# One token tile through a precomputed low-rank product, fewer and longer unread matmuls, and later values: one change in three parts to an attention-and-mixer kernel

## The chip, the cores and the metric

The kernel runs on one core of a Trainium2 chip. The metric is the device time of one execution in microseconds (us), as a median over several executions. Before the change it is 313.06 us (three runs, 312.72 to 313.33). All times below that come from a trace are counted from the first instruction of the profiled execution. The trace's span is about 1.7 us shorter than the device time of the same execution (311.4 for 313.08).

## The reference

Sliding-window causal attention, then a mixer with a low-rank product over the tokens and a two-layer MLP over the channels:

```python
# q, k, v: (8, 8, 576, 64); window 64
scores = scale * q @ k.T                       # masked to 0 <= i - j < 64
x = softmax(scores) @ v                        # -> (8, 576, 512)
xt = x.transpose(0, 2, 1)
h = xt @ U @ V                                 # U: (576, 32), V: (32, 576)
u = x + h.transpose(0, 2, 1)
out = u + np.maximum(u @ w_ch1, 0.0) @ w_ch2   # 512 -> 2048 -> 512
```

The 576 tokens of a batch are handled as five tiles, four of 128 tokens and one of 64.

## The kernel before

The MLP needs u with the channels on the partitions ("d-major"), and the last addition needs it with the tokens on the partitions. For batch 0 the d-major u is made on TensorE in four PSUM banks, one for 128 channels each: XT transposes x into them and HT adds the low-rank product. `hh` is U'x, made by UM in one bank (`psh` for batch 0, `pshh` for the others) and cast by ScalarE.

```python
def UM(ts):                                    # hh = U' x over the token tiles ts
    def f():
        ...                                    # tiles 0-3: two matmuls each, two column groups
        ...                                    # tile 4: four matmuls, each half the columns
        if ts[-1] == NT - 1:
            hh["sb"] = wk_pool.tile([P, CH], BF16, name="hh", tag="hh")
            for cs in (slice(0, CH // 2), slice(CH // 2, CH)) if spare else (slice(0, CH),):
                nc.scalar.copy(out=hh["sb"][:, cs], in_=hh["ps"][:, cs])
    return f

def bank(dc):                                  # the PSUM bank of channel block dc
    if dc not in ua:
        if dc < 2:
            ua[dc] = psum["mm"].tile([P, CH], FP32, name="uam", tag="mm")[:]
        elif dc == 2:
            ua[dc] = ps_tp.tile([P, CH], FP32, name="uat", tag="tp")[:]
        else:
            ua[dc] = ps_big.tile([P, 2, CH], FP32, name="uab", tag="big")[:, 0, :]
    return ua[dc]

def HT(dcs):                                   # called with (0, 1), then (2, 3)
    def f():
        for n, dc in enumerate(dcs):
            half = slice(n * 2 * R, (n + 1) * 2 * R)
            nc.tensor.matmul(bank(dc), hh["sb"][half, dc * P : (dc + 1) * P],
                             vrep[half, W : W + CH], start=False, stop=True)
        for dc in dcs:
            copy = nc.scalar.copy if dc % 2 == 0 else nc.vector.tensor_copy
            copy(out=uT_of(b)[:, :, dc, :], in_=bank(dc).rearrange(...))
    return f
```

The program begins with matmuls whose results nobody reads. They are there to raise TensorE's clock while the first loads are under way (its record goes from half to full at 6.03 us in this trace). Then come batch 0's attention and mixer, and from then on the MLP of one batch with the attention and mixer of the next one spread over its numbered slots:

```python
PLACE_0 = {"V": [0, 0, 1, 2, 2, 3, 4, 4, 4]}   # batch 0's token-major values of u (psv)
PLACE_1 = {..., "SV": [18, 18, 19, 19], "PV": [20], "U": [25], "V": [26, 31], ...}
...
turn_over(62, 96)                              # 62 unread matmuls of 96 columns
...                                            # batch 0: scores, head tiles
a["R"](); ...                                  # values of tiles 0, 1
a["PV"][2](); spread_v(3, nc.scalar.copy)
a["XT"][0](); a["XT"][1]()
a["PV"][3](); a["U"][0]()
a["PV"][4](); a["U"][1]()
for t in range(2, NFULL):
    a["XT"][t](); a["U"][t]()
for f in [a["U"][NT - 1]] + a["X3"] + a["HT"]:
    f()
```

SV copies batch 1's V into place, PV computes its attention values, U its hh.

The softmax here doesn't subtract the row's maximum and nothing guards it: scores larger than these inputs give would overflow.

Of the kernel before, what the change touches and what calls it, by code (L numbers as in the profile page):

```python
# [11 lines left out]
BF16 = mybir.dt.bfloat16  # L12
FP32 = mybir.dt.float32
# [3 lines left out]
def kernel(  # L17
# [11 lines left out]
    nc = tc.nc  # L29
    B, H, S, D = q.shape  # L30
    DM = H * D
    R = moe_U.shape[1]
    F = moe_w_ch1.shape[1]
    P = nc.NUM_PARTITIONS
    W = 64
    NB = S // W
    HP = H // 2
    NDC = DM // P
# [7 lines left out]
    NFULL = S // P  # L46
    CH = 512
# [11 lines left out]
    const = ctx.enter_context(tc.tile_pool(name="const", bufs=1))  # L59
# [3 lines left out]
    wk_pool = ctx.enter_context(tc.tile_pool(name="wk", bufs=2))  # L63
# [17 lines left out]
    NT = 5  # L81
# [2 lines left out]
    vrep = const.tile([P, W + S + W], BF16, name="vrep")  # L84
    vf = const.tile([R, S], FP32, name="vf")
    idle = const.tile([P, CH], BF16, name="idle")
    xs = [const.tile([P, NT, H, D], BF16, name=f"xs{i}") for i in range(2)]
    vA = [const.tile([P, NFULL, H, VW], BF16, name=f"vA{i}") for i in range(2)]
    vB = [const.tile([P, NFULL, H, VW], BF16, name=f"vB{i}") for i in range(2)]
# [60 lines left out]
    def shift_low(b, copy, t):  # L150
# [9 lines left out]
        out=ident[:],  # L160
        in_=ident[:],
# [27 lines left out]
    nc.vector.memset(vrep[:, W + S : W + S + W], 0.0)  # L189
    nc.vector.memset(uf[0][:, NT - 1, :], 0.0)  # L190
    nc.vector.memset(xs[0][W:P, NT - 1, :, :], 0.0)
    nc.vector.memset(xs[1][0:W, 0, :, :], 0.0)
    for i in range(2):
        nc.vector.memset(kn[i][GP:P, NFULL, :, :], 0.0)
# [27 lines left out]
    def spread_v(g, copy):  # L222
        copy(out=vrep[g * R : (g + 1) * R, W : W + S], in_=vf[:])
# [8 lines left out]

    def load_rest():
        load_w1(1024, 2048)
        for g in range(3):
            spread_v(g, nc.gpsimd.tensor_copy)
        for _ in load_kq(1, False):
            pass
        w2v = moe_w_ch2.rearrange("(i p) m -> p i m", p=P)
        for i in range(0, NFC, 4):  # L240
            if i == NFC - 4:
                load_v(1)
            nc.gpsimd.dma_start(out=w2b[:, i : i + 4, :], in_=w2v[:, i : i + 4, :])
# [10 lines left out]
    def attention(b, spare=False):  # L254
# [262 lines left out]
        hh = {}  # L517
        xc = lambda src, t, dc: src[:, t, :, :].rearrange("p h d -> p (h d)")[:, dc * P : (dc + 1) * P]

        def UM(ts):  # L520
            def f():
                if ts[0] == 0:
                    if spare:
                        hh["ps"] = psum["spare"].tile([P, CH], FP32, name="psh", tag="spare")
                    else:
                        hh["ps"] = ps_big.tile([P, 2, CH], FP32, name="pshh", tag="big")[:, 0, :]
                for t in ts:
                    xt = x[:, t, :, :].rearrange("p h d -> p (h d)")
                    if t < 4:
                        for g in (t % 2, t % 2 + 2):  # L530
                            nc.tensor.matmul(  # L531
                                hh["ps"][g * R : (g + 1) * R, :], ub[odd][:, t, :], xt,
                                start=(t < 2), stop=False,
                            )
                        continue

                    for g in range(4):
                        cols = slice((g % 2) * CH // 2, (g % 2 + 1) * CH // 2)
                        nc.tensor.matmul(  # L539
                            hh["ps"][g * R : (g + 1) * R, cols], ub[odd][:, t, :], xt[:, cols],  # L540
                            start=False, stop=True,
                        )
                if ts[-1] == NT - 1:
                    hh["sb"] = wk_pool.tile([P, CH], BF16, name="hh", tag="hh")
                    for cs in (slice(0, CH // 2), slice(CH // 2, CH)) if spare else (slice(0, CH),):
                        nc.scalar.copy(out=hh["sb"][:, cs], in_=hh["ps"][:, cs])  # L546
            return f


# [3 lines left out]
        def bank(dc):  # L553
            if dc not in ua:
                if dc < 2:
                    ua[dc] = psum["mm"].tile([P, CH], FP32, name="uam", tag="mm")[:]
                elif dc == 2:
                    ua[dc] = ps_tp.tile([P, CH], FP32, name="uat", tag="tp")[:]
                else:
                    ua[dc] = ps_big.tile([P, 2, CH], FP32, name="uab", tag="big")[:, 0, :]  # L560
            return ua[dc]

        opened = []
# [13 lines left out]
        def XT(t, dcs):  # L577
            def f():
                opened.append(t)
                for dc in dcs:  # L580
                    cols = bank(dc)[:, t * P : (t + 1) * P]

                    nc.tensor.matmul(cols, xc(x, t, dc), ident[:], start=(t == 0), stop=False)
            return f

        def HT(dcs):
            def f():
                for n, dc in enumerate(dcs):
                    half = slice(n * 2 * R, (n + 1) * 2 * R)
                    nc.tensor.matmul(  # L590
                        bank(dc),
                        hh["sb"][half, dc * P : (dc + 1) * P],
                        vrep[half, W : W + CH],
                        start=False,
                        stop=True,
                    )
                for dc in dcs:
                    copy = nc.scalar.copy if dc % 2 == 0 else nc.vector.tensor_copy
                    copy(  # L599
                        out=uT_of(b)[:, :, dc, :],  # L600
                        in_=bank(dc).rearrange("p (t q) -> p t q", q=P),
                    )
            return f
# [63 lines left out]
            pcs["M"] = [MK(j) for j in range(HP)]  # L667
            pcs["M"].insert(0 if b >= NGR else HP, MK8)
        pcs["PV"] = [PVA] if not spare else [None, None] + [PV(t) for t in range(2, NT)]
        pcs["U"] = [UM((t,)) for t in range(NT)] if spare else [UM(tuple(range(NT)))]  # L670
        if spare:
            pcs["L"] = [PVL(t) for t in range(2)]
            pcs["R"] = PVR
            pcs["XT"] = [XT(t, range(NDC - 1)) for t in range(NFULL)]
            pcs["idle"] = idle_turns
            pcs["X3"] = [XT(t, (NDC - 1,)) for t in range(NFULL)]
            pcs["HT"] = [HT((0, 1)), HT((2, 3))]
            pcs["V"] = [f for ts in ((0, 1), (2, 3), (4,)) for f in VM(ts)]
        else:
            def two_banks():  # L680
                return (
                    psum["mm"].tile([P, CH], FP32, name="psv0", tag="mm"),
                    ps_tp.tile([P, CH], FP32, name="psv1", tag="tp"),
                )

            def mixed(parts=None):
                parts = parts or [VM((NT - 1,), two_banks), VM((0, 1)), VM((2, 3))]
                for part in parts:
                    part[0]()
                for part in parts:  # L690
                    for add in part[1:]:
                        add()

            pcs["V"] = [mixed]
            if b == 1:

                def last():
                    for f in VM((NT - 1,)):
                        f()

                pcs["V"] = [lambda: mixed([VM((0, 1)), VM((2, 3))]), last]
            pcs["UT"] = [UT(t) for t in range(NT if odd else NT - 1)]
# [6 lines left out]
    def mlp(c):  # L709
# [83 lines left out]
        "V": [16],  # L793
        "UT": [17, 17, 18, 18, 19],
    }
    PLACE_0 = {"V": [0, 0, 1, 2, 2, 3, 4, 4, 4]}
    PLACE_1 = {
        "T": [11, 11, 12, 12, 14, 14, 15, 15],
        "S": [12, 13, 15, 16, 16],
        "M": [13, 14, 16, 17, 17],  # L800
        "SV": [18, 18, 19, 19],
        "PV": [20],
        "U": [25],
        "V": [26, 31],
        "UT": [28, 29, 30, 31, 102],
# [21 lines left out]
    def turn_over(n, cols, rows=P):  # L827
        for _ in range(n):
            nc.tensor.matmul(
                unread[0:rows, 0:cols], idle[:, 0:rows], idle[:, 0:cols], start=True, stop=True  # L830
            )


    turn_over(62, 96)
    att = {0: attention(0, spare=True)}
    a = att[0]
    nc.vector.tensor_scalar(
# [27 lines left out]
    for what in order.split():  # L865
        j = int(what[1])
        if what[0] in "SBL":
            a[what[0]][j]()
        else:
            a["T"][2 * j + (what[0] == "Q")]()  # L870
        if what == "Q1":
            load_low_rank()
            nc.scalar.copy(out=ub[0][:], in_=uf[0][:])
        if what in ("Q1", "Q3"):
            turn_over(1, CH)
    load_rest()
# [2 lines left out]
    shift_low(0, nc.scalar.copy, 2)  # L879
    a["idle"](1)  # L880
    a["PV"][2]()
    spread_v(3, nc.scalar.copy)
    a["XT"][0]()
    a["XT"][1]()
    a["PV"][3]()
    a["U"][0]()
    a["PV"][4]()
    a["U"][1]()
    for t in range(2, NFULL):
        a["XT"][t]()  # L890
        a["U"][t]()
    load_low_rank_1()
    for f in [a["U"][NT - 1]] + a["X3"] + a["HT"]:
        f()
    repeat(nc.vector.tensor_copy, maskA[:, 0])
    nc.vector.tensor_copy(out=maskA[:, 1, :, :], in_=maskA[:, 0, :, :])
# [7 lines left out]
    for c in range(NCH):  # L904
        slots = all_slots[c]

        def place(b, parts, where):
            if b not in att:
                att[b] = attention(b)
            for part in parts:  # L910
                for f, s in zip(att[b][part], where[part]):
                    all_slots[c + s // 100][s % 100].append(f)

        b = c + 1
        if b < B:
# [20 lines left out]
            if b < NXB:  # L936
                place(b, ("T",), where)
            if b == 1:
                place(0, ("V",), PLACE_0)
                slots[6].append(lambda: nc.scalar.copy(out=ub[1][:], in_=uf[1][:]))  # L940
            if 3 < b + 1 < B:
                slots[24].append(lambda bs=b + 1: shift_v(bs, nc.vector.tensor_copy))
# [57 lines left out]
```

## Time and profile before

| | before |
|---|---|
| median of 3 runs | 313.06 us |
| span of the trace | 311.4 us |
| TensorE (PE) busy | 303.9 us, 98% |
| first transposing product into u (XT) | 16.45 us |
| first low-rank product into u (HT) | 20.74 us |
| first MLP matmul (psA) | 21.80 us |
| batch 1's first pshh (U1) | 51.61 us |

The page says that TensorE is the limit; the five times are read from TensorE's timeline and are the milestones. Each stretch between two of them is a stage. Two lines of TensorE's waits in the first 64 us (for whom it waited; us in total, times, longest) show that in the stage before psA there were two waits of 0.4 us, one on ScalarE's cast of u and one on nothing that the profile shows ("issue"):

```profile
PE psA L724 <- ACT uTc L599: 0.4, 1, 0.4
PE psh L539 <- issue: 0.4, 1, 0.4
```

ScalarE's timeline of the kernel before (start, us, instruction) has the two copies of V on which batch 0's value tile 3 depends; they end at 16.79:

```profile
15.49 0.62 ACT L148 COPY vB<-vA 64x520 bf16<-64x520 bf16 x1
16.17 0.62 ACT L151 COPY vB<-vA 64x520 bf16<-64x520 bf16 x1
```

### The profile page before, as it was taken

How to read it: one execution, taken by the hardware profiler on the slowest of the kernel's cores; microseconds unless marked ns; L12 is line 12 of the kernel's file. 1: busy time of each engine (PE TensorE's matmuls, PEld its weight loads, DVE VectorE, ACT ScalarE, POOL GpSimd, SP SyncE). 2: the span in 40 equal slices, each digit the busy share in tenths (PEclk: the TensorE clock that was granted, in tenths of full speed). 3: DMA queues.
4: the chain of work that ended last, by engine and by line, in shares of the span. 5: the costliest groups of instructions: out<-in, count | busy, mean ns of one | idle time of the engine just before them, and what ended most of it. 6: DMA issues, size and time to landing. Idle time of an engine off the chain costs nothing.

```text
span 311.4 us, 6970 instructions
## 1 busy us (share of the span) xinstructions
PE 303.9 (98%) x2897; PEld 148.4 (48%) x2919; DVE 161.8 (52%) x308; ACT 108.8 (35%) x173; POOL 101.7 (33%) x133
## 2 busy tenths in 40 slices
PE   8989999999999999999999999999999999999996
PEld 7643554544455544453445344544454444444443
DVE  4665467437758753774368435844574343016011
ACT  3745670467038510642063304340345003201500
POOL 8693263293497097029308710000000000000000
PEclk9999999999999999999999999999999999999999
DMA  7999999999999999999999999515100545010012
GB/s 108 167 210 208 205 168 147 145 148 154 129 150 140 126 152 156 182 161 159 163 155 207 150 106 181 128 48 133 69 2 0 120 180 193 27 76 34 0 64 73
DMA packets 156496, 39.88 MB, mean 128 GB/s; under 512 B 145040, under 2 KB 151440, under 8 KB 156464
## 3 DMA queue, kind: packets, MB, share of 16 engines
q0 software_dynamic: 104720, 18.88, 87.3%
q1 hardware_dynamic: 51744, 20.55, 35.0%
q8 instruction: 23, 0.38, 0.5%
q14 instruction: 9, 0.07, 0.1%
HBM read 37.97 MB, written 9.44 MB: 152 GB/s over the span
## 4 chain that ended last, share of the span: by engine, by line
PE 93%; DMA 3%; POOL 2%; issue 1%; ACT 0%; DVE 0%; POOLq 0%
PE psA L724 41%; PE psU L748 40%; DMA vA<-in_v_dram 3%; PE sc L345 3%; PE xw L407 2%; PE psv L619 2%; PE pshh L531 1%; PE tpu L653 1%; PE tpg L281 0%; POOL qr L119 0%; PE low L345 0%; PE psh L531 0%; POOL vB L151 0%; PE xr L407 0%; POOL kr L119 0%
## 5 line engine op out<-in xcount | busy, mean ns | idle before, releaser
L724 PE MATMUL psA<-uTc,w1b 128*128 128x512 bf16 (+1 forms) x580 | 131.2, 378 | 0.4 <-ACT uTc L599 0.4
L748 PE MATMUL psU<-w2b,c 128*128 128x512 bf16 (+2 forms) x572 | 127.5, 373 | 1.3 <-issue 0.3
L748 PEld LDWEIGHTS <-c 128*128 128x128 bf16 x592 | 56.0, 98 | 66.4 <-issue 3.6
L724 PEld LDWEIGHTS <-w1b 128*128 128x128 bf16 x580 | 54.1, 98 | 64.4 <-issue 2.9
L736 ACT ACTIVATE c<-psA 128x512 bf16<-128x512 f32 x84 | 50.0, 597 | 88.3 <-PE psA L724 88.0
L761 DVE TENSOR_TENSOR osb<-psU,un 128x512 f32<-128x512 f32 (+2 forms) x29 | 19.5, 672 | 69.3 <-PE psU L748 69.3
L734 DVE TENSOR_SCALAR c<-psA 128x512 bf16<-128x512 f32 x60 | 41.3, 688 | 25.6 <-PE psA L724 25.6
L634 DVE TENSOR_TENSOR un<-psv,xs 128x512 bf16<-128x512 f32 (+3 forms) x48 | 26.1, 592 | 23.5 <-PE psv L619 23.3
L365 ACT ACTIVATE pts<-sc 128x1024 bf16<-128x1024 f32 x32 | 31.4, 1028 | 2.3 <-PE sc L345 2.3
L137 POOL DMA_DIRECT2D vA<-in_v_dram x32 | 28.5, 915 | 8.1 <-DMA w1b<-in_moe_w_ch_dram 2.8
L128 POOL DMA_DIRECT2D qr<-in_q_dram x30 | 26.7, 890 | 4.5 <-DMA w2b<-in_moe_w_ch_dram 3.1
L128 POOL DMA_DIRECT2D kr<-in_k_dram x30 | 26.7, 890 | 4.1 <-PE psA L724 2.0
L398 ACT ACTIVATE ptl<-low 128x256 bf16<-128x256 f32 x6 | 2.3, 384 | 62.0 <-PE high L345 62.0
L371 DVE TENSOR_TENSOR pts<-pts,maskA 128x1024 bf16<-128x1024 bf16 x28 | 19.1, 682 | 1.7 <-ACT pts L365 1.7
L922 POOL COPY held<-qf 1x1 bf16<-1x1 bf16 x5 | 1.1, 228 | 54.0 <-DMA qf<-qr 54.0
L498 DVE TENSOR_TENSOR xs<-xw,rcw 128x896 bf16<-128x896 f32 x14 | 15.3, 1091 | 0.5
L345 PEld LDWEIGHTS <-kf 64*64 64x64 bf16 x704 | 9.9, 107 | 7.7 <-issue 7.0
L345 PE MATMUL sc<-qf,kf 64*64 64x128 bf16 (+1 forms) x608 | 11.7, 212 | 0.5 <-DVE qf L298 0.3
L407 PEld LDWEIGHTS <-pts 128*64 128x64 bf16 x512 | 9.9, 110 | 3.7 <-issue 3.2
L546 ACT CAST hh<-pshh 128x512 bf16<-128x512 f32 x7 | 4.1, 586 | 13.7 <-PE pshh L539 13.5
L656 ACT COPY uTc<-tpu 128x512 bf16<-128x512 bf16 x9 | 5.3, 585 | 10.2 <-PE tpu L653 10.2
L407 PE MATMUL xw<-vA,pts 128*64 128x65 bf16 x217 | 8.4, 195 | 0.0
(115 smaller groups left out, 175.3 us busy)
## 6 DMA issues: line engine op xcount, KB each, us to landing
out_dram<-osb SPq DMA_DIRECT2D x27, 256.0 KB, 2.3
vA<-in_v_dram POOLq DMA_DIRECT2D x32, 128.0 KB, 8.1
kr<-in_k_dram POOLq DMA_DIRECT2D x24, 128.0 KB, 5.8
qr<-in_q_dram POOLq DMA_DIRECT2D x24, 128.0 KB, 6.4
w2b<-in_moe_w_ch_dram POOLq DMA_DIRECT2D x4, 512.0 KB, 15.0
out_dram<-late SPq DMA_DIRECT2D x8, 256.0 KB, 3.0
vB<-in_v_dram POOLq DMA_DIRECT2D x8, 128.0 KB, 12.3
w1b<-in_moe_w_ch_dram POOLq DMA_DIRECT2D x2, 512.0 KB, 11.5
```

The lines of the kernel that those rows point to most:

```text
L128: nc.gpsimd.dma_start(out=dst[0:rows, t, :, :], in_=src[b, :, t * P : t * P + rows, :].rearrange("h p d -> p h d"),)
L137: nc.gpsimd.dma_start(out=dst[:, :, 0:D], in_=v[b, :, lo : lo + P, :].rearrange("h p d -> p h d"))
L345: nc.tensor.matmul(sc[g][r0 : r0 + W, col * W : (col + n) * W], keys_of(j, u, rs), queries_of(j, blk, n, rs), start=not spare, stop=last o ...
L365: nc.scalar.activation(out=dst, in_=sc[:], func=ACT.Exp, scale=scale)
L371: nc.vector.tensor_tensor(out=dst, in0=dst, in1=maskA.rearrange("p g n w -> p g (n w)"), op=ALU.mult)
L407: nc.tensor.matmul(dst, pts[:, h // 2, h % 2, blk, :] if blk < NB - 1 else ptl[:, h // 2, h % 2, :], rhs, start=True, stop=True,)
L634: nc.vector.tensor_tensor(out=u_tiles[g][rs, cs], in0=ps[0][n][rs], in1=x[rs, t, :, :].rearrange("p h d -> p (h d)")[:, cs], op=ALU.add,)
L724: nc.tensor.matmul(ps[i][:, ts.start * P : ts.stop * P], w1b[:, dc, i * P : (i + 1) * P], uTc[:, ts, dc, :], start=(dc == 0), stop=(dc == ...
L734: nc.vector.tensor_relu(out=c1[i][:], in_=ps[i][:])
L736: nc.scalar.activation(out=c1[i][:], in_=ps[i][:], func=ACT.Relu)
L748: nc.tensor.matmul(acc[t][:, lo:hi], c1[i][:, t * P : (t + 1) * P], w2b[:, i, lo:hi], start=(i == 0), stop=(i == NFC - 1),)
L761: nc.vector.tensor_tensor(out=osb[:, lo:hi], in0=acc[t][:, lo:hi], in1=u_tiles[g][:, lo:hi], op=ALU.add,)
```

## The change

The intent is to start the MLP earlier. hh of batch 0's first four tiles no longer waits for the fifth, because the last tile's share of the low-rank product, its U times V, is made once from the weights alone (`m4`) and multiplied with the last tile of x. hh over all five tiles is still needed for the token-major values, so UM runs once more in the MLP's slot 0. The unread matmuls become fewer and longer, which leaves fewer instructions ahead of the kernel proper. Batch 1's values go one slot later.

```diff
-        def UM(ts):
+        def UM(ts, early=False):
...
+                if early and ts[-1] == NFULL - 1:
+                    hh["four"] = wk_pool.tile([P, CH], BF16, name="hh4", tag="hh4")
+                    for cs in (slice(0, CH // 2), slice(CH // 2, CH)):
+                        nc.scalar.copy(out=hh["four"][:, cs], in_=hh["ps"][:, cs])
...
-                elif dc == 2:
-                    ua[dc] = ps_tp.tile([P, CH], FP32, name="uat", tag="tp")[:]
                 else:
-                    ua[dc] = ps_big.tile([P, 2, CH], FP32, name="uab", tag="big")[:, 0, :]
+                    pair = ps_big.tile([P, 2, CH], FP32, name="uab", tag="big")
+                    ua[2], ua[3] = pair[:, 0, :], pair[:, 1, :]
...
+        def mix_last():
+            ps = ps_tp.tile([P, CH], FP32, name="psm", tag="tp")
+            for n in range(W // R):
+                rs = slice(n * R, (n + 1) * R)
+                nc.tensor.matmul(ps[rs, :], u4t[rs, :], vrep[rs, W : W + CH], ...)
+            nc.scalar.copy(out=m4[0:W, :], in_=ps[0:W, :])
...
         def HT(dcs):
...
-                        hh["sb"][half, dc * P : (dc + 1) * P],
+                        hh["four"][half, dc * P : (dc + 1) * P],
...
                 for dc in dcs:
+                    nc.tensor.matmul(
+                        bank(dc), xc(x, NT - 1, dc), m4[:], start=False, stop=True
+                    )
                     copy = nc.scalar.copy if dc % 2 == 0 else nc.vector.tensor_copy
...
-    PLACE_0 = {"V": [0, 0, 1, 2, 2, 3, 4, 4, 4]}
+    PLACE_0 = {"U": [0], "V": [2, 2, 3, 4, 4, 5, 6, 6, 6]}
...
-        "SV": [18, 18, 19, 19],
-        "PV": [20],
+        "SV": [19, 19, 20, 20],
+        "PV": [21],
...
-    turn_over(62, 96)
+    turn_over(40, 149)
...                                  # load_rest spreads V's copies in another order
-    a["U"][0]()
+    a["U4"][0]()
     a["PV"][4]()
-    a["U"][1]()
-    for t in range(2, NFULL):
-        a["XT"][t]()
-        a["U"][t]()
+    a["mix"]()
+    a["U4"][1]()
+    a["XT"][2]()
+    a["U4"][2]()
+    a["U4"][3]()
+    a["XT"][3]()
     load_low_rank_1()
-    for f in [a["U"][NT - 1]] + a["X3"] + a["HT"]:
+    for f in a["X3"] + a["HT"]:
         f()
```

The matmul added in HT is called a tail below.

More of the change, by code (lines that the diff above doesn't have):

```diff
@@ L86 @@
     idle = const.tile([P, CH], BF16, name="idle")
+    u4t = const.tile([W, R], BF16, name="u4t")
+    m4 = const.tile([P, CH], BF16, name="m4")
     xs = [const.tile([P, NT, H, D], BF16, name=f"xs{i}") for i in range(2)]
@@ L191 @@
     nc.vector.memset(xs[0][W:P, NT - 1, :, :], 0.0)
+    nc.vector.memset(m4[W:P, :], 0.0)
     nc.vector.memset(xs[1][0:W, 0, :, :], 0.0)
@@ L234, in load_rest @@
         load_w1(1024, 2048)
-        for g in range(3):
+        for g in (0, 2, 3):
             spread_v(g, nc.gpsimd.tensor_copy)
@@ L518, in attention @@
         xc = lambda src, t, dc: src[:, t, :, :].rearrange("p h d -> p (h d)")[:, dc * P : (dc + 1) * P]
-        def UM(ts):
+        def UM(ts, early=False):
             def f():
                 if ts[0] == 0:
-                    if spare:
+                    if early:
                         hh["ps"] = psum["spare"].tile([P, CH], FP32, name="psh", tag="spare")
@@ L532, in f @@
                                 hh["ps"][g * R : (g + 1) * R, :], ub[odd][:, t, :], xt,
-                                start=(t < 2), stop=False,
+                                start=(t < 2), stop=(early and t >= 2),
                             )
@@ L542, in f @@
                         )
+                if early and ts[-1] == NFULL - 1:
+                    hh["four"] = wk_pool.tile([P, CH], BF16, name="hh4", tag="hh4")
+                    for cs in (slice(0, CH // 2), slice(CH // 2, CH)):
+                        nc.scalar.copy(out=hh["four"][:, cs], in_=hh["ps"][:, cs])
                 if ts[-1] == NT - 1:
                     hh["sb"] = wk_pool.tile([P, CH], BF16, name="hh", tag="hh")
-                    for cs in (slice(0, CH // 2), slice(CH // 2, CH)) if spare else (slice(0, CH),):
-                        nc.scalar.copy(out=hh["sb"][:, cs], in_=hh["ps"][:, cs])
+                    nc.scalar.copy(out=hh["sb"][:], in_=hh["ps"][:])
             return f
@@ L584, in XT @@
             return f
+        def mix_last():
[3 more added lines that the diff above has]
+                nc.tensor.matmul(
+                    ps[rs, :], u4t[rs, :], vrep[rs, W : W + CH], start=True, stop=True
+                )
+            nc.scalar.copy(out=m4[0:W, :], in_=ps[0:W, :])
         def HT(dcs):
@@ L591, in f @@
                         bank(dc),
-                        hh["sb"][half, dc * P : (dc + 1) * P],
+                        hh["four"][half, dc * P : (dc + 1) * P],
                         vrep[half, W : W + CH],
                         start=False,
-                        stop=True,
+                        stop=False,
                     )
                 for dc in dcs:
+                    nc.tensor.matmul(
+                        bank(dc), xc(x, NT - 1, dc), m4[:], start=False, stop=True
+                    )
                     copy = nc.scalar.copy if dc % 2 == 0 else nc.vector.tensor_copy
@@ L669, in attention @@
         pcs["PV"] = [PVA] if not spare else [None, None] + [PV(t) for t in range(2, NT)]
-        pcs["U"] = [UM((t,)) for t in range(NT)] if spare else [UM(tuple(range(NT)))]
+        pcs["U"] = [UM(tuple(range(NT)))]
+        pcs["U4"] = [UM((t,), True) for t in range(NFULL)]
         if spare:
@@ L673, in attention @@
             pcs["R"] = PVR
-            pcs["XT"] = [XT(t, range(NDC - 1)) for t in range(NFULL)]
+            pcs["XT"] = [XT(t, (0, 1)) for t in range(NFULL)]
+            pcs["mix"] = mix_last
             pcs["idle"] = idle_turns
-            pcs["X3"] = [XT(t, (NDC - 1,)) for t in range(NFULL)]
+            pcs["X3"] = [XT(t, (2, 3)) for t in range(NFULL)]
             pcs["HT"] = [HT((0, 1)), HT((2, 3))]
@@ L873 @@
             nc.scalar.copy(out=ub[0][:], in_=uf[0][:])
+            nc.vector.transpose(out=u4t[:], in_=ub[0][0:W, NT - 1, :])
         if what in ("Q1", "Q3"):
@@ L881 @@
     a["PV"][2]()
-    spread_v(3, nc.scalar.copy)
+    spread_v(1, nc.scalar.copy)
     a["XT"][0]()
@@ L938 @@
             if b == 1:
-                place(0, ("V",), PLACE_0)
+                place(0, ("U", "V"), PLACE_0)
                 slots[6].append(lambda: nc.scalar.copy(out=ub[1][:], in_=uf[1][:]))
```

## The prediction

> **What bounds the kernel now.** I read the page first, then the chain of waits in order of time, then the timelines of TensorE, VectorE and ScalarE over the first 62 us.
>
> The page's busy times and its chain by engine:
>
> ```profile
> PE 303.9 (98%) x2897; PEld 148.4 (48%) x2919; DVE 161.8 (52%) x308; ACT 108.8 (35%) x173; POOL 101.7 (33%) x133
> ...
> PE 93%; DMA 3%; POOL 2%; issue 1%; ACT 0%; DVE 0%; POOLq 0%
> ...
> q8 instruction: 23, 0.38, 0.5%
> ```
>
> TensorE is busy 98% of the span and is 93% of the chain. So a matmul added after the start costs its full time, and there is little to win but the few idle pieces. The third line, the instruction queue, matters below.
>
> The chain in order of time, around the start (start, us, what):
>
> ```profile
> 6.16 7.85 DMA vA<-in_v_dram
> 14.06 0.61 POOL vB L151
> 14.73 0.62 POOL vB L148
> 15.40 0.62 POOL vB L151
> 16.07 0.45 PE xr L407 x16
> 21.18 0.58 ACT uTc L599
> 21.80 1.89 PE psA L724 x8
> ```
>
> Up to 16.07 the end is set by loading V and by three GpSimd copies, not by TensorE. From 21.80, when the first MLP matmul (psA) starts, TensorE is gapless. The change can act in the 5.73 us between, and through TensorE work or waits after them. The TensorE timeline of that stretch:
>
> ```profile
> 18.62 0.39 PE L531 MATMUL psh<-xs,ub 128*32 128x512 bf16 x2
> 18.94 0.28 PE L583 MATMUL uam<-ident,xs 128*128 128x128 bf16 x2
> 19.07 0.22 PE L583 MATMUL uat<-ident,xs 128*128 128x128 bf16 x1
> 19.21 0.39 PE L531 MATMUL psh<-xs,ub 128*32 128x512 bf16 x2
> 19.97 0.29 PE L539 MATMUL psh<-xs,ub 128*32 128x256 bf16 x4 [0.36 <-issue]
> 20.19 0.40 PE L583 MATMUL uab<-ident,xs 128*128 128x128 bf16 x4
> 20.74 0.39 PE L590 MATMUL uam<-vrep,hh 64*128 64x512 bf16 x2
> 21.02 0.39 PE L590 MATMUL uat<-vrep,hh 64*128 64x512 bf16 x1
> 21.02 0.39 PE L590 MATMUL uab<-vrep,hh 64*128 64x512 bf16 x1
> 21.80 1.89 PE L724 MATMUL psA<-uTc,w1b 128*128 128x512 bf16 x8 [0.40 <-ACT uTc L599]
> ```
>
> A pair of psh matmuls runs together and the next kind starts 0.32 after it (18.62 to 18.94). The last token tile's psh starts at 19.97, not at 19.21 + 0.32 = 19.53: 0.44 lost to "issue". Its input was ready, since VectorE ended that tile's xs at 18.51 + 0.68 = 19.19, and even its weight load, which waits for no semaphore, starts only at 19.97. In the compiled list this is PE row 703. Counting 64 rows of prologue (my guess) makes row 704 = 3 x 256 - 64 a fetch-block edge, so I read the 0.44 as waiting for instructions. Then the products uam wait for the cast hh, and psA for hh products and the cast uTc.
>
> **What the Trainium skill says.**
> - "Runtime: NRT & Kernel Launch", Instruction fetch mechanics: instructions come in 16 KiB blocks of 256, and crossing an edge is mostly hidden. The trace agrees on the size (0.38 MB in 23 fetches is 16.5 KB each). On hidden, this case differs once, by 0.44 us, if my reading holds.
> - "TensorEngine Tiling (Array Packing)", Key Properties: changing the tiling mode drains TensorE. The trace agrees: a pair of 512-column matmuls ahead of another shape takes 0.32 where one such matmul takes 0.216 (13.81 us for 64 psA on the chain), so about 0.1 per switch.
> - "TensorE: Matmul & The Clock Gate", What's actually happening: the array starts at half its 2.4 GHz. The 62 unread matmuls of 96 columns take 4.96 us (1.26 to 6.22), 80 ns each, which is 96 / 1.2 GHz: agrees.
>
> **The change part by part.**
>
> 1. *40 unread matmuls of 149 columns for 62 of 96.* 5,960 columns for 5,952: at half clock 4.97 us for 4.96, so the start stays. What it does do is take 44 rows out of TensorE's list, which moves the edge at row 704 from the early chain to the first re-done U matmul in MLP slot 0, reached some 3 us later. The 0.44 goes.
>
> 2. *Early chain from 16.07.* Walking the new list with the old steps:
>  - the transposing products XT of tiles 0 and 1 have 4 matmuls, not 6 (-0.11), but value tile 3 waits for a ScalarE copy ending 16.17 + 0.62 = 16.79, so it moves from 16.94 to 16.86 only: -0.08.
>  - The mixing product, two matmuls at once, adds 0.32.
>  - U of tiles 2 and 3 are now adjacent and use four column groups at once: -0.32.
>  - U of tile 4 is gone (0.22) and with it the 0.44.
>  - The ScalarE cast of the product now starts after tile 3's U (18.81 + 0.39, so about 19.25) and its first half is ready at 19.67, while TensorE does ten more XT until 19.79. The old wait 20.37 to 20.74 shrinks to one switch: -0.22.
>  - Then pair, two tail matmuls (0.22 each), pair, two tail matmuls: 19.79, 20.12, 20.34, 20.65, 20.97, 21.20, done issuing at 21.41. Four 512-column tail matmuls are the price (0.86) plus two switches.
>  - The first cast uTc runs 20.55 to 21.14, before TensorE needs it, so the old wait before psA (21.02 + 0.31 to 21.80, 0.47) is filled with work.
>  psA starts at about 21.41 for 21.80: **-0.39**. The later casts (21.46, 22.00, 22.31) are ahead of their matmuls (21.84, 22.27, 22.70).
>
> 3. *U of batch 0 done once more in slot 0* (8 + 4 matmuls), for the token-major values. The same group for batch 1 shows the cost:
>
> ```profile
> 50.65 1.03 PE L748 MATMUL psU<-w2b,c 128*128 128x512 bf16 x4
> 51.61 0.62 PE L531 MATMUL pshh<-xs,ub 128*32 128x512 bf16 x8
> 52.05 0.28 PE L539 MATMUL pshh<-xs,ub 128*32 128x256 bf16 x4
> 52.27 1.04 PE L748 MATMUL psU<-w2b,c 128*128 128x512 bf16 x4
> ```
>
>  Four psU from 50.65 would let the next start at 50.65 + 4 x 0.216 = 51.51; it starts at 52.27: **+0.75**, all on the path, as TensorE is gapless there.
>
> 4. *The first psv waits for hh.* psA pair ends issuing at 23.13, U at 23.88, psA 2 at 24.75; psv could start at 24.85. ScalarE evicts c 0 and 1 from 23.33 (1.0 for two, as 23.72 to 24.81 minus the tail), then casts hh until 24.91: psv at about 24.97, **+0.12**. Moving V from slots 0, 2, 4 to 2, 4, 6 costs nothing else.
>
> 5. *Batch 1's values one slot later (slot 21), while its U stays at slot 25.* VectorE's chain behind the values:
>
> ```profile
> 47.17 0.18 DVE L487 RECIPROCAL rce<-xe 128x4 f32<-128x4 f32 x1 [1.78 <-PE xe L407]
> ...
> 50.28 0.17 DVE L506 RECIPROCAL rco<-one 128x4 f32<-128x4 f32 x1
> 50.48 0.86 DVE L510 TENSOR_TENSOR xs<-one,rco 64x256 bf16<-64x256 f32 x2
> ```
>
>  It ends at 51.34, U's first matmul waits for exactly that last op (tile 0 of batch 1 is filled last) and starts at 51.61: with 0.05 for the semaphore there is 0.22 to spare. One slot less between values and U takes away four psU, 4 x 0.216 = 0.86. So a new wait of 0.86 - 0.22 = **+0.65**. What the move buys, more time for V's loads and copies, was worth nothing in this trace: values started at 45.90 with the usual switch gap.
>
> Sum: -0.39 + 0.75 + 0.12 + 0.65 = **+1.13 us**, 313.06 to 314.2.
>
> **Rivals.**
> - *The early gain carries.* If everything after psA absorbed the additions, the time would be 312.7. For it: the intent. Against: TensorE idles 0.32 us in all from 40 to 60 us (19.68 busy of 20), so 0.75 of new matmuls has nowhere to hide.
> - *The VectorE wait at batch 1's U does not come* (the wait is on an earlier op than I think, or the chain starts earlier): 313.5. Against: the compiled list has that matmul wait for VectorE, and the chain's order is unchanged.
> - *Instruction fetch becomes the wait elsewhere.* The edge now falls in slot 0; if the fetch is asked for only when the first psA is released (21.4), and takes the 2.3 us that it took before (17.64 to 19.97), up to 0.5 comes back: 314.7. Against: rows 664 to 703 are read some 2 us earlier than that.
> - *A load becomes the bound.* V of batch 1 lands at 45.06; with TensorE about 0.5 later and values a slot later it has 1.3 us more room. This makes no time, only less scatter.
>
> **Range and chances.** The two large terms, 0.75 and 0.65, are read from the same trace at nearly the same place; the early term rests on a walk of some fifteen steps, each good to a few hundredths, so +-0.3. The three runs before spread over 0.6 us. I take 314.2, with 313.2 to 315.0. Two per cent is 6.3 us, six times the largest sum I can form, so "within 2%" is near certain.
>
> **What would show it.** Right if: unread still ends near 6.22; no "issue" gap near 19.5; psA starts near 21.4; twelve pshh matmuls follow at about 23.2; the first psv waits about 0.1 on ScalarE; and pshh of batch 1 shows a wait of about 0.65 on VectorE's xs. From there to the end the distances should equal the old ones. Wrong if psA starts before 21.0 or after 21.8 (the walk missed a wait), if pshh of batch 1 shows no wait, or if an issue gap stands at slot 0.

## The result, and the profile after

The changed kernel takes **316.5 us** (six runs, 315.68 to 318.39) where the kernel before took 312.84 in six runs. A ratio here and below is the mean time of one kernel's fast runs over that of the other's of the same rounds, so it is not quite the ratio of the medians: 1.0124, with a 95% interval of 1.0093 to 1.0156. The class "within 2%" was right; the range 313.2 to 315.0 did not hold the time. The profiled execution is the fastest of the six, 315.68 us with a span of 314.0.

The page of the changed kernel, busy times and chain by engine: TensorE's own work has grown by 0.9 us only, and VectorE and ScalarE now stand in the chain with 1% each, where the page before gave them 0%.

```profile
PE 304.8 (97%) x2888; PEld 148.2 (47%) x2911; DVE 162.9 (52%) x310; ACT 110.0 (35%) x175; POOL 101.9 (32%) x133
PE 92%; DMA 2%; DVE 1%; ACT 1%; issue 1%; POOL 1%; POOLq 0%
```

The waits of TensorE in the first 64 us name three that the kernel before did not have:

```profile
PE uab L612 <- ACT uTc L616: 0.7, 1, 0.7
PE pshh L534 <- DVE xs L513: 0.6, 1, 0.6
PE xr L410 <- ACT vB L153: 0.3, 1, 0.3
```

The second was predicted (0.65). The others were not. TensorE's timeline of the same trace shows where they lie, and a small "issue" gap at the first head values:

```profile
14.51 0.22 PE L410 MATMUL xh<-vA,pts 128*64 128x65 bf16 x3 [0.23 <-issue]
...
17.41 0.19 PE L410 MATMUL xr<-vB,pts 128*64 128x65 bf16 x1 [0.33 <-ACT vB L153]
...
21.20 0.39 PE L604 MATMUL uab<-vrep,hh 64*128 64x512 bf16 x2
21.52 0.39 PE L612 MATMUL uab<-m,xs 128*128 128x512 bf16 x1
22.59 0.38 PE L612 MATMUL uab<-m,xs 128*128 128x512 bf16 x1 [0.67 <-ACT uTc L616]
22.80 1.89 PE L743 MATMUL psA<-uTc,w1b 128*128 128x512 bf16 x8
```

The two tails of the second HT are at 21.52 and 22.59, 1.07 apart where two adjacent ones are 0.22 apart. Between them lies ScalarE's cast of the bank that the first tail filled. ScalarE's timeline of the changed kernel: the cast runs from 21.95 to 22.53, and the second tail starts 0.06 later. The copy of V now ends at 17.35, and value tile 3 starts 0.06 after it.

```profile
15.47 0.60 ACT L401 ACTIVATE ptl<-sc 128x512 bf16<-128x512 f32 x1 [0.30 <-PE sc L348]
...
16.73 0.62 ACT L153 COPY vB<-vA 64x520 bf16<-64x520 bf16 x1
...
21.95 0.58 ACT L616 CAST uTc<-uab 128x512 bf16<-128x512 f32 x1 [0.27 <-PE uab L612]
```

The milestones of every trace, in us. "A to U1" is the stretch from the end of the last psA matmul of the first eight (0.22 after its start) to batch 1's first pshh; "edge" is the step from the matmul before to the one at row 447 to 449 of TensorE's compiled list. With 62 unread matmuls this is a change from one tiling of the array to another, and the same change takes 0.31 in all thirteen traces. With 40 or 50 it is in the middle of a group, whose matmuls otherwise follow each other within 0.05.

| kernel | unread | XT | XT to HT | HT to psA | psA | A to U1 | U1 to end | span | edge |
|---|---|---|---|---|---|---|---|---|---|
| before | 62 | 16.45 | 4.29 | 1.06 | 21.80 | 28.08 | 259.8 | 311.4 | 0.31 |
| before_again | 62 | 17.03 | 3.86 | 1.06 | 21.94 | 28.09 | 259.8 | 311.5 | 0.31 |
| after | 40 | 16.68 | 3.66 | 2.46 | 22.80 | 29.68 | 259.8 | 314.0 | 0.42 |
| after_again | 40 | 17.01 | 3.84 | 2.46 | 23.31 | 30.10 | 260.6 | 315.8 | 0.73 |
| a1_tails_first | 40 | 16.77 | 3.84 | 1.62 | 22.23 | 29.60 | 259.9 | 313.7 | 0.57 |
| a2_old_slots | 40 | 17.00 | 3.84 | 2.46 | 23.30 | 30.27 | 261.1 | 316.4 | 0.85 |
| a3_unread62 | 62 | 16.63 | 3.64 | 2.46 | 22.73 | 29.60 | 259.8 | 313.8 | 0.31 |
| a4_own_banks | 40 | 16.90 | 3.69 | 1.62 | 22.21 | 29.60 | 259.8 | 313.3 | 0.71 |
| b1_unread40 | 40 | 17.27 | 4.21 | 1.06 | 22.54 | 28.08 | 260.0 | 312.3 | 0.71 |
| b2_later_slot | 62 | 16.73 | 3.74 | 1.06 | 21.53 | 28.74 | 259.8 | 311.8 | 0.31 |
| b3_redo_u | 62 | 16.23 | 4.04 | 1.06 | 21.33 | 28.95 | 259.8 | 311.8 | 0.31 |
| b4_unread50 | 50 | 17.24 | 4.01 | 1.06 | 22.31 | 28.08 | 259.8 | 311.9 | 1.20 |
| c3_three_undone | 62 | 17.01 | 3.52 | 1.62 | 22.15 | 28.95 | 259.8 | 312.6 | 0.31 |

For the profiled pair: U1 is 2.60 later (54.21 for 51.61), and so is the end. That is 1.00 before psA and 1.60 between psA and U1. After U1 nothing has changed.

### The profile page after: what moved, and what is told of

It reads as the page before. It is cut to its first block, busy times and chain, and to the rows that moved or that the text cites. A ratio compares the mean times of both kernels' runs of the same rounds, so it can differ in the third digit from the quotient of the medians.

```text
span 314.0 us, 6958 instructions
## 1 busy us (share of the span) xinstructions
PE 304.8 (97%) x2888; PEld 148.2 (47%) x2911; DVE 162.9 (52%) x310; ACT 110.0 (35%) x175; POOL 101.9 (32%) x133
## 4 chain that ended last, share of the span: by engine, by line
PE 92%; DMA 2%; DVE 1%; ACT 1%; issue 1%; POOL 1%; POOLq 0%
PE psA L743 41%; PE psU L767 39%; PE sc L348 3%; DMA qr<-in_q_dram 2%; PE xw L410 2%; PE psv L636 2%; PE pshh L534 1%; PE tpu L670 1%; DVE xs L501 1%; PE tpg L284 1%; PE low L348 0%; POOL kr L121 0%; PE tpw L284 0%; PE psh L534 0%; PE xe L410 0%
## 5 line engine op out<-in xcount | busy, mean ns | idle before, releaser
L139 POOL DMA_DIRECT2D vB<-in_v_dram x8 | 7.4, 926 | 3.7 <-DMA qr<-in_q_dram 2.7
```

The lines of the kernel that those rows point to most:

```text
L139: nc.gpsimd.dma_start(out=dst[:, :, 0:D], in_=v[b, :, lo : lo + P, :].rearrange("h p d -> p h d"))
```

## The experiments

Labels a1 to a4 are edits of the changed kernel, b1 to b4 of the kernel before, and c3 is several edits at once. Each was run on a chip beside the kernel before in the same rounds, and every one gave the reference's result. The theory to be tested was threefold: that the missing time before psA is (A) a wait that the shared tile of two banks makes, (B) a stall for instructions at an edge of the fetch blocks, which the smaller number of unread matmuls has moved to a worse place, and that (C) re-done U and later slot cost what was predicted. The rival to A was that TensorE's tails wait for something else (the casts as such, or the product m4); the rival to B, that the gaps come from the new instructions of the early chain and have nothing to do with the unread matmuls.

### A: the second pair of banks

**a1_tails_first**: both tails ahead of both copies.

```diff
                     nc.tensor.matmul(
                         bank(dc), xc(x, NT - 1, dc), m4[:], start=False, stop=True
                     )
+                for dc in dcs:
                     copy = nc.scalar.copy if dc % 2 == 0 else nc.vector.tensor_copy
```

> The changed kernel with the four tail matmuls no longer mixed with the copies: in each pair both tails come before both copies. Theory (shared pair): the last tail waited 0.84 us for the ScalarE cast of the other half of the same two-bank PSUM pair; with the order turned round that wait is gone, psA starts about 0.8 us earlier after the first uam product, and the time falls by about 0.8 us against the changed kernel (about 315.7 for 316.5). Rival (the casts bound psA anyway): psA's later matmuls wait for the casts instead, the time falls by under 0.2 us.

Measured: 315.61 us (315.28 to 315.9, four runs), ratio 1.0078 (1.0062 to 1.0094). From HT to psA it takes 1.62, as the prediction had walked it. The timeline of TensorE for this kernel shows the two tails as one group:

```profile
21.79 0.61 PE L612 MATMUL uab<-m,xs 128*128 128x512 bf16 x2
22.23 1.46 PE L744 MATMUL psA<-uTc,w1b 128*128 128x512 bf16 x6
```

But the first eight psA matmuls take 1.99 where they take 1.72 elsewhere, as the casts now start later and their readers wait. VectorE's cast of the second half of the tile does not start until ScalarE's cast of the first has ended (23.05 after 23.02; the trace names ScalarE as what it waited for). With the two banks apart, in a4 below, it starts at 22.41, while ScalarE's still runs (22.20 to 22.78). So 0.27 of the 0.84 is given back. The order of the instructions makes the wait; whether the tile does was for the next one.

**a4_own_banks**: the old loop, but the third and fourth bank are two tiles again.

```diff
+                elif dc == 2:
+                    ua[dc] = ps_tp.tile([P, CH], FP32, name="uat", tag="tp")[:]
                 else:
-                    pair = ps_big.tile([P, 2, CH], FP32, name="uab", tag="big")
-                    ua[2], ua[3] = pair[:, 0, :], pair[:, 1, :]
+                    ua[dc] = ps_big.tile([P, 2, CH], FP32, name="uab", tag="big")[:, 0, :]
```

> The changed kernel with the third and fourth token-column bank in two different PSUM tiles, as before, in place of one pair. Theory (shared pair): the whole wait goes, without the 0.27 us that the first fix (copies after both tails) gave back inside psA; from the first uam product to the end of the first psA pair it is 3.44 us in place of 4.28, and the time falls by about 0.8 us against the changed kernel on this chip. Rival (the casts bind): 3.7 or more remains, as with the first fix, and the time falls by 0.5 us.

Measured: 315.41 us (314.76 to 316.96, six runs), ratio 1.0062 (1.0022 to 1.0101). The changed kernel itself had 1.0118 in the same rounds (after_again). TensorE's timeline has the tails of the two banks back to back, with the copy between them in the program as in the changed kernel:

```profile
21.77 0.39 PE L613 MATMUL uat<-m,xs 128*128 128x512 bf16 x1
22.00 0.38 PE L613 MATMUL uab<-m,xs 128*128 128x512 bf16 x1
22.21 1.46 PE L744 MATMUL psA<-uTc,w1b 128*128 128x512 bf16 x6
```

HT to psA is 1.62 and the eight psA are at their 1.72. In the trace's record the second of these tails waits for a semaphore in the changed kernel and for none in this one. So the wait needs both: one tile for two banks, and a reader of the one between the writers. A write into one half of a tile waits here for the reader of the other half, and in a1 one reader waited for the other. Theory A stands: 0.84 us. The tails as such and m4 are excluded, since neither was changed. The times of these rounds fell by more than the trace accounts for (1.9 us between the medians), but their intervals overlap and settle nothing beyond it.

### B: the unread matmuls and the edge of the fetch blocks

**b1_unread40**: the kernel before, with `turn_over(40, 149)` for `turn_over(62, 96)`, and nothing else.

> The kernel before with only the unread matmuls changed to 40 of 149 columns. Theory (instruction fetch): the idle 0.36 us marked issue ahead of the last tile's U is gone, psA starts about 0.4 us earlier and the time falls by about 0.4 us (to about 312.4), with the old small scatter. Rival (clock): runs scatter by 2 us or more and the median rises by 1 us or so, as then the shorter list alone explains the part of the loss that the profiled run of the changed kernel does not show.

Measured: 313.67 us (313.3 to 314.04, five runs), ratio 1.0013 (0.9997 to 1.0028). By time alone this is no certain loss; the expected fall of 0.4 us did not come, and neither did the rival's scatter of 2 us. The trace shows the stall at the same place as the changed kernel's, the first head values, with none of the new instructions in the program:

```profile
15.28 0.22 PE L407 MATMUL xh<-vA,pts 128*64 128x65 bf16 x3 [0.51 <-issue]
```

**a3_unread62**: the changed kernel with `turn_over(62, 96)`.

> The changed kernel with the 62 unread matmuls of 96 columns back. Theory (the scatter of 315.7 to 318.4 comes from the shorter list of unread matmuls, through the clock or the instruction fetch): the six runs lie within 0.7 us of each other as before's do, and the median falls by about 1 us; against it, the fetch edge would fall into the tile products and cost up to 0.4. Rival (the scatter has another cause, loads or the new order): the scatter stays at 2 us and the median stays within 0.5 us.

Measured: 315.72 us (315.53 to 316.01, four runs), ratio 1.0083 (1.0067 to 1.0098). No stall at this edge or at the two later ones before U1. Its psA is only 0.07 earlier than in the changed kernel's first trace, whose stall was the smallest of all with 40 (a step of 0.42, where a3's at these values are 0.05 at most), as Q came later in a3 (ScalarE's last copy of it at 12.35 for 12.07); against the second trace it is 0.58 earlier. The expectation came out in the numbers, with four runs within 0.48 us and a ratio lower by 0.4%. But a1, with 40 unread matmuls and in the same rounds, has its four runs within 0.62, so the scatter of the changed kernel is not pinned on their number.

**b4_unread50**: the kernel before with `turn_over(50, 119)`, an attempt at a version that beats it.

> The kernel before with 50 unread matmuls of 119 columns: 24 rows fewer, so the edges of the instruction blocks fall at rows 448 and 704 of a list in which row 448 is in the scores of the last head pair and row 704 in the first psA. Theory (edges): no idle piece at either the values or the last tile's U; the chain from the first tile product to the first uam product is 3.74 us, and the time is equal to or up to 0.3 us under the kernel before. Rival (the stalls do not go by rows): an idle piece marked issue stays at the last tile's U or at the first values.

Measured: 313.8 us (313.63 to 314.44, six runs), ratio 1.0026 (1.0014 to 1.0038), so a little slower. The expectation missed: the edge fell among the last head pair's scores, which I took for harmless, and TensorE stalled there for longer than anywhere with 40:

```profile
14.78 0.25 PE L345 MATMUL sc<-qf,kf 64*64 64x128 bf16 x5 [0.98 <-issue]
```

What B comes to: the stall follows the row of the list, not the kind of instruction. It is at row 447 or 449 in all seven traces with 40 or 50 unread matmuls, in old and new kernels alike. Of the six with 62, five have none. The first trace of the kernel before lost 0.16 just there: its 18 scores from 13.30 take 0.58, where those of before_again, from 13.49, take 0.42. So with 62 the edge is less exposed, not harmless. In the trace's records of the instruction queue the first fetch is asked for at 11.7 to 12.6 us with 40 and 50, at 10.1 to 10.9 with 62, and the stalled instruction starts 2.5 to 3.1 us after the asking. The one trace with 62 that stalled asked last of the six (10.94), and TensorE came to the row 2.4 us later; in the other five it came 2.7 to 3.5 us after the asking. A fetch that is asked for too late fits all of it. Why it is asked for later was only argued (the asking seems to follow TensorE's progress in the list, and fewer unread rows put it behind a wait for the Q load); no run separates it. How much time the stall makes varies with when Q, K and V land, as later waits may swallow it.

### The kernels once more: after_again and before_again

Both are unedited, to see what one execution shows by chance.

> The changed kernel once more, unedited, for its scatter and for the same chip as the next three. Theory (the slow ones of its runs meet late instruction blocks and late loads at random): again a lowest time near 315.5, a median near 316 and single runs 1 to 2 us above the rest; in its trace an idle piece marked issue stands at row 447 of TensorE's list (the first values, at 14.5 to 15.0). Rival (the first measurement was off): all runs within 0.6 us of each other near 315.

Measured: 317.29 us (316.21 to 318.68, six runs), ratio 1.0118 (1.0079 to 1.0158); two of the six runs had a mean clock of 0.994 to 0.995 and took 318.6. The profiled run (span 315.8, clock 1.0) has the wait of A at the same 2.46, but 0.73 at the first edge, 0.50 where the next edge falls in batch 1's scores (0.07 in the first trace), and a wait that neither first trace had, at 129 us, on transposes of u that the DMA queues deliver:

```profile
129.09 1.02 PE L743 MATMUL psA<-uTc,w1b 128*128 128x512 bf16 x4 [0.69 <-DMA uTc<-un]
```

> The kernel before once more, unedited, for a second trace. If the 0.44 us stall at row 703 is bound to rows and to how early the block is asked for, it is there again when the block is asked for after 17.5 us and is small when it is asked for before 17.3, as in the two kernels whose first 703 rows are the same (0.15 and 0.20 us there). Rival: it is always there at 0.44.

Measured: 313.22 us, one run; its span is 311.5. Its literal expectation of a repeated stall missed: the last token tile's psh follows its neighbour without a gap, although its block was asked for at 17.61, as in the first trace (17.64).

```profile
19.90 0.39 PE L531 MATMUL psh<-xs,ub 128*32 128x512 bf16 x2
19.98 0.43 PE L539 MATMUL psh<-xs,ub 128*32 128x256 bf16 x4
```

From asking to that instruction it is 2.37 us here and was 2.33 in the first trace. There TensorE came to the place early and waited; here V had landed later, TensorE came 0.69 later (19.90 for 19.21), and the same fetch was hidden. From token tile 3's psh to the XT behind tile 4's it is 0.98 in the first trace (19.21 to 20.19) and 0.44 here (19.90 to 20.34); b2_later_slot and b3_redo_u, whose lists are the same up to there, have 0.43 to 0.44 as well. So the stall was 0.54 rather than the prediction's 0.44, which allowed 0.32 for a change of tiling between the two psh, and both have the same tiling. And it is no fixed loss of the kernel before: it shows when TensorE gets ahead of the fetch. An early V alone does not make it, since b3's landed earlier still (XT at 16.23) and its block, asked for at 17.12, came in time. psA was at 21.80 with the stall and at 21.94, 21.53 and 21.33 without.

### C: the re-done U and the later slot

**b2_later_slot**: the kernel before with batch 1's values at the new slots.

```diff
-        "SV": [18, 18, 19, 19],
-        "PV": [20],
+        "SV": [19, 19, 20, 20],
+        "PV": [21],
```

> The kernel before with one thing of the change alone: batch 1's shifts and values one slot later. Theory (VectorE chain): a wait of about 0.65 us for VectorE stands ahead of batch 1's U and the time rises by 0.65 us. Rival (it is free in the kernel before, or it saves a wait for V's loads in some runs): the time stays within 0.3 us.

Measured: 313.7 us (313.37 to 314.66, six runs), ratio 1.0001 (0.9967 to 1.0035). These rounds can't show 0.2%: two of the kernel before's eleven runs took 315.2 and 316.1. The trace can. A to U1 is 28.74 for 28.08, **+0.66**, and TensorE's timeline has the wait:

```profile
51.99 0.62 PE L531 MATMUL pshh<-xs,ub 128*32 128x512 bf16 x8 [0.54 <-DVE xs L510]
```

The 0.54 is idle time alone, counted from the modelled end of the matmul ahead; from start to start the stage grew by 0.66.

**b3_redo_u**: the kernel before, with U of batch 0 run once more in slot 0 and its values two slots later.

```diff
+        pcs["U2"] = [UM(tuple(range(NT)))]
...
-    PLACE_0 = {"V": [0, 0, 1, 2, 2, 3, 4, 4, 4]}
+    PLACE_0 = {"U2": [0], "V": [2, 2, 3, 4, 4, 5, 6, 6, 6]}
```

> The kernel before with one thing of the change alone: batch 0's U done a second time in slot 0 and its values in slots 2, 4 and 6, with the early chain as it was. Theory (TensorE has no room there): the time rises by 0.75 us for the twelve matmuls plus about 0.1 us for the first psv's wait on the cast, 0.85 in all. Rival (some of it is hidden in later waits): under 0.5 us.

Measured: 313.93 us (313.47 to 314.68, six runs), ratio 1.0008 (0.9974 to 1.0043); the same scatter. The trace: A to U1 is 28.95 for 28.08, **+0.87**. TensorE's timeline has the twelve matmuls of U where the kernel before has its first psv:

```profile
23.14 0.61 PE L531 MATMUL pshh<-xs,ub 128*32 128x512 bf16 x8
23.59 0.28 PE L539 MATMUL pshh<-xs,ub 128*32 128x256 bf16 x4
23.80 1.04 PE L725 MATMUL psA<-uTc,w1b 128*128 128x512 bf16 x4
```

**a2_old_slots**: the changed kernel with the old slots of batch 1's values (b2's edit undone).

> The changed kernel with batch 1's shifts and values back in their old slots (18, 18, 19, 19 and 20). Theory (VectorE chain): the wait of 0.66 us ahead of batch 1's U goes, its first matmul again shows the plain switch gap of 0.31, and the time falls by about 0.65 us (to about 315.9). Rival (values then wait for V's loads): a new wait of some tenths stands ahead of the values and the time falls by under 0.3 us.

Measured: 316.23 us (315.7 to 318.1, six runs), ratio 1.0105 (1.0083 to 1.0128). The expected 0.65 is not seen in the time. The profiled run was the slowest of the six, so its trace is no fair sample: the wait on VectorE is gone from it, but at the edge in batch 1's scores it lost 1.12, and at 129.72 it waited 1.16 for the same transposes as after_again. A to U1 less the whole step of 1.32 at that edge is 28.95, which is the re-done U alone.

```profile
45.84 0.25 PE L348 MATMUL sc<-qf,kf 64*64 64x64 bf16 x7 [1.12 <-issue]
```

### Three parts undone together

**c3_three_undone**: the changed kernel with a4's banks, a2's slots and a3's unread matmuls. What stays is the product m4 in the early chain and the re-done U.

> The changed kernel with three parts taken back at once: two separate banks in place of the pair, batch 1's values in their old slots, 62 unread matmuls of 96 columns. What is left of the change is the product of the low-rank factors in the early chain and the U done again. If the parts add up: no wait on a cast before psA, 1.62 us from the first uam product to psA, 28.95 us from the end of the first psA pair to batch 1's U, no idle piece at row 447; time about 1.2 us over the kernel before (ratio 1.004), about 2.3 us under the changed kernel. Rival (something else of the change costs as well): ratio 1.007 or more.

Measured: 314.13 us (313.72 to 314.3, five runs), ratio 1.0031 (1.0019 to 1.0043). Trace: A to U1 28.95, HT to psA 1.62, no stall at an edge. The parts add up: what is left is 0.87 for U, and psA 0.21 later than in before_again, whose V landed at a like time (XT at 17.01 and 17.03); together 1.08 for spans of 312.6 and 311.5. So even without its three mishaps the change gains nothing in the early chain, as far as one pair of traces can tell. No version tried beats the kernel before.

## Why the prediction was wrong

Take the prediction's sum, +1.13, to the 2.60 of the profiled pair:

- **Part 1, the unread matmuls: wrong.** "The 0.44 goes" had nothing to take: the stall was in one of the four traces that have this row at this place, and psA came at about the same time in the others. The edge that mattered was the one before it, 256 rows up, which I never placed. Taking out 44 rows (22 matmuls with their weight loads) moved it from the scores, where it cost 0.16 in one trace of six and nothing in five, to the head values, where 0.4 to 0.8 was lost in all six traces with 40. "The start stays" held for the end of the K load, not for the unread matmuls: they took 4.42 where the same view shows 5.03 for the old ones, with the clock full at 4.74 us in that execution and at 6.03 in the old one.
- **Part 2, the early chain: the failed step with the largest term.** The sentence "The later casts (21.46, 22.00, 22.31) are ahead of their matmuls" asked whether psA waits for the casts, and not whether a *tail* does. I had read the new pair of banks as two banks, and it is one tile. HT to psA was 1.62 in the walk and 2.46 on the chip, **+0.84**; a4 gives back exactly 1.62. The prediction's own sign of a missed wait, psA after 21.8, came true.
- **Part 2, value tile 3: mis-sized.** The walk had it at 16.86, behind a ScalarE copy ending at 16.79. The copy ended at 17.35 and the tile started at 17.41, **+0.55**. ScalarE's timeline splits it: its copy of the last Q tiles (qf) came 0.35 later than before (12.07 for 11.72), as the load had landed later, and it then waited 0.30 for the scores behind the stalled edge, less 0.1 of small differences between the two traces. From 17.41 on the walk was right to a hundredth up to HT: 2.93 in both.
- So psA came at 22.80 where 21.41 was predicted: 1.39, the 0.84 and the 0.55.
- **Parts 3 and 4: right.** 0.75 + 0.12 = 0.87 predicted; 0.87 in b3, and in c3 and a2 too.
- **Part 5: right.** 0.65 predicted, 0.66 in b2. With part 3 and 4, A to U1 is 29.60, 1.52 above the old 28.08, in a1, a3 and a4; the changed kernel's 0.08 more is the edge in batch 1's scores, a step of 0.07 for about none.
- **The rival "Instruction fetch becomes the wait elsewhere"** was the right kind of fear at the wrong edge: slot 0 shows no issue gap. "The early gain carries" and "the VectorE wait does not come" fell with b3 and b2, which show both additions in full.

1.13 + 0.84 + 0.55 + 0.07 + 0.01 = 2.60. The time of the six runs shows more: a ratio of 1.0124 is 3.9 us. The profiled run was the fastest of them. The second pair of traces shows some of what the others have: its span is 4.3 us longer than before_again's, of which 1.37 before psA, 2.01 between psA and U1 (1.53 for parts 3 to 5 and 0.5 at the edge) and 0.85 after U1, most of it the late transposes. That these losses come more often with the change is what the medians suggest, but only two traces of the changed kind have the late transposes, and **why they are late stays open**, as does the share of runs in which the mean clock is 0.99: such runs came up for the kernel before as well. The range of +-0.9 around a walk of fifteen steps took the scatter of the kernel before (0.6 us) for that of the new one.

The lesson in the terms themselves: -0.39 for the early chain was -0.44 for a stall that one execution showed and +0.05 for everything else; with the step put right it is -0.54 and +0.15, and c3, without the stall, measured +0.21. The second execution of the kernel before shows the first term to be absent, and with it the whole intended gain.

## What to carry to other kernels

When a change puts two banks into one tile, ask for every write into one half which engine reads the other half just before it in program order; the compiled list names that wait, and moving the bank to a tile of its own takes it away. Before taking credit for a gap, look for it in a second execution, and place *every* edge of the instruction stream, not the one that happens to show. A stage's time between two milestones, in the trace, decides parts of 0.2% that rounds of time can't.

## What the Trainium skill lacked or had wrong

- "Runtime: NRT & Kernel Launch", Instruction fetch mechanics: that crossing a block's edge is mostly hidden is too kind for a short early stage. At TensorE's rows 447 to 449 all seven traces with 40 or 50 unread matmuls show a step of 0.42 to 1.20 us where 0.05 at most is usual, and at the edge in batch 1's scores two of them show 0.50 and 1.32. The page does not say how long a block takes: 2.3 to 3.1 us from asking to the first stalled instruction here. Where the edges fall, 192 rows past a multiple of 256 in these lists (448, 704, 1216), is in no page.
- "TensorE: Matmul & The Clock Gate", What you observe: the clock rises around 4 us into sustained work, give or take 0.5. Here the first unread matmul starts at 1.26 in every trace and the clock record goes full at 4.17 to 7.13, that is after 2.9 to 5.9 us, more scatter than the half microsecond of that sentence.
- "TensorEngine Tiling (Array Packing)", Key Properties: changing the tiling mode drains TensorE, without a size. Here about 0.1 us: in the changed kernel's trace it is 0.31 to 0.32 from a 512-column matmul, or two at once, to another tiling, and 0.22 from a 512-column one to a 128-column one of the same tiling.
- No page has it that a write into one bank of a tile of two can be made to wait for a reader of the other bank: 0.84 us here. This is the program's bookkeeping rather than the chip's: the wait is for a semaphore, and it is gone in a4.
